# A fused attention and gated-MLP kernel on one core: the hand-written order of all engines replaced by another

## The chip, the core and the metric

The kernel runs on one core of a Trainium2 chip. The metric is device time in microseconds, from the first to the last instruction of an execution as the device counts it, median of several runs. Engines are named as in the profile: PE (TensorE) multiplies matrices, DVE (VectorE), ACT (ScalarE) and POOL (GpSimd) work on elements, SP (SyncE) issues DMA transfers. Each engine executes its own instructions in the order in which the program lists them, and waits on semaphores where it needs another's result.

## What is computed

A block-wise linear attention with decay for 4 batches, 8 heads, 768 tokens and head width 64, and behind it a gated MLP with a spatial projection. Cut to what matters:

```python
# attention: per head, blocks of 64 tokens, state kv carried from block to block
intra = ((qb @ kb.T) * Dmask) @ vb
inter = (qb * lam_pow) @ kv
out   = intra + inter
kv    = lam_block * kv + (kb * rev_pow).T @ vb
# gMLP on x = attention output as (batch, 768, 512)
h    = relu(x @ w_in)                  # 512 -> 1024
u, v = h[..., :512], h[..., 512:]
v_n  = (v - mean(v)) / sqrt(var(v) + 1e-6)
v_s  = w_spatial @ v_n + b_spatial     # over the 768 tokens
y    = (u * v_s) @ w_out               # 512 -> 512
```

## The kernel before

The work is cut into 12 pieces n of 256 tokens, three to a batch (n = 0 to 2 are batch 0). A piece goes through the attention, is turned into the MLP's input and projected. When the three pieces of a batch are there, the spatial product of that batch can run, and then its output product. The kernel has no loop over this: a string `ORDER` lists 675 tokens, and for each the function of that name is called. The last letter says the engine (T PE, D DVE, A ACT, P POOL, S SP), the numbers say which piece, half or bank. As the tokens are listed, so each engine executes its share; the framework adds the semaphores where one token needs another's data or buffer. PSUM has 8 banks; most tokens name the bank they use, and bank 7 keeps the attention state.

```python
for token in ORDER.split():
    name, *args, e = token.split(".")
    ops[name](e, *map(int, args))
```

The tokens, in the order of the flow:
- LK, LQ, LV n (`load`, L193): one piece of k, q or v from HBM, 512 KB, by SP into one of three buffers. WI, WS (`w_in`, `w_sp`, L249 and L254, two halves each), WO (L258): weights, issued by POOL with conversion to bf16. BS (L261): the bias. GT (`after`, L245): POOL copies one element of a loaded piece, and so waits for its landing; it holds back the weights behind it.
- KM, QM (`decay`, L291): k or q times its decay, half a piece each, on DVE or POOL. QC, VC: conversion of q and v to bf16. In n = 0 to 4, TK and TQ (`tr`, L321) transpose k and q on PE and EK, EQ bring the result to SBUF (EQ with the decay, L335); later pieces go through DMA transposes by SP (DK, DQ; L304, L308) instead. EQ is written for DVE whatever its letter:

```python
def e_q(e, n, x, b):
    nc.vector.tensor_tensor(...)
```

- SC (L352) makes the scores on PE, MK (L357) masks them on DVE; KV (L369) adds to the state, SS copies it out; AV (L390, L399) makes the attention output; FN reads one element of it; EX brings it out as the MLP's input.
- PV (L424) and PU (L462) are the two halves of the first projection on PE; EV and EU (`relu`) their evictions. BN (L439, L440), RA (L444), RD (L449) and VN (L453) normalise v; VN is on DVE throughout, bf16 from SBUF to SBUF.
- WT (L474) transposes w_spatial on PE once, EW evicts it. GP puts the bias into a bank, PW (L488) adds the spatial product to it (32 tokens of 6 matmuls; each needs all six VN of its batch), GM (L494) multiplies by u. PO (L499) is the output product of 128 tokens, EO its eviction, ST its store; PH, EH and SH do the last such tile in halves.
- FL (`f_l`, L269): k matmuls of w columns on a constant tile into a bank that is written anew afterwards. They compute nothing that is used.

At the start, `lam` is brought in, LB, LN, LL, LX and LT make the decay factors from it, msk, mkc, idn, posk, pos and one make masks and constants.

In the order before, 86 fillers of 256 columns stand in 12 groups ahead of the first spatial product PW.0.0.0. The weights stand on POOL as WI.0 behind GT.1.1 (q of n = 1), WI.1 behind GT.1.2 (q of n = 2), WS.0 behind GT.2.1 (v of n = 1), WO behind GT.2.2 (v of n = 2), with KM, QC and VC between them. SP's queue begins K0, Q0, K1, Q1, V0, V1, Q2, K2, V2, BS, K3, Q3, V3, K4, Q4.

Of the kernel before, what the change touches and what calls it, by code (L numbers as in the profile page):

```python
# [36 lines left out]
KV.3.0.T SC.3.0.0.1.T MK.3.0.0.1.D SC.3.1.2.3.T MK.3.1.2.3.D GP.0.2.1.4.A PW.0.2.1.4.T TK.4.2.6.T QC.4.2.A
TQ.4.2.5.T EQ.4.2.5.D GM.0.2.1.4.D GP.0.3.1.0.A PW.0.3.1.0.T AV.3.0.1.2.T FN.3.1.2.D SS.3.0.A KV.3.1.T KM.5.1.P
EK.4.2.6.A SC.4.0.3.4.T GM.0.3.1.0.D KM.5.0.D DK.5.S AV.3.1.1.2.T EX.3.1.2.A EX.3.0.1.A SC.4.1.5.6.T
MK.4.1.5.6.D PO.0.2.0.T EO.0.2.0.A PO.0.4.2.T EO.0.4.2.D QM.5.1.P QM.5.0.D DQ.5.S VC.5.P PO.0.3.1.T PU.3.0.5.T  # L40
PV.3.1.6.T PV.3.0.0.T VC.4.A SS.3.1.D KV.4.0.T MK.4.0.3.4.D AV.4.0.2.3.T EV.3.0.0.D BN.3.0.D PO.0.5.4.T
EU.3.0.5.A SS.4.0.A KV.4.1.T EV.3.1.6.A BN.3.1.D LK.6.S KM.6.0.P FN.4.2.3.A AV.4.1.2.3.T EX.4.1.3.D SS.4.1.A
LV.6.S EX.4.0.2.A RA.3.A RD.3.D PO.0.1.0.T EO.0.1.0.A EO.0.3.1.A KV.5.0.T SC.5.0.5.6.T MK.5.0.5.6.D SC.5.1.2.3.T
MK.5.1.2.3.D SS.5.0.A PO.0.0.0.T EO.0.0.0.A LQ.6.S QM.6.0.P PV.4.1.1.T PV.4.0.5.T LK.7.S KM.7.0.P LQ.7.S
KM.6.1.D VN.3.0.D LQ.8.S DK.6.S EO.0.5.4.A AV.5.0.2.6.T FN.5.2.6.D PU.4.0.3.T EV.4.1.1.A EV.4.0.5.A QM.6.1.P
AV.5.1.2.6.T BN.4.0.D VC.6.A KV.6.0.T GP.1.2.0.0.D EX.5.0.2.D PU.4.1.4.T EU.4.0.3.A EX.5.1.6.A EU.4.1.4.A
VN.3.1.D BN.4.1.D PV.5.1.1.T EV.5.1.1.D RA.4.A RD.4.D BN.5.1.D PV.5.0.5.T LV.7.S EV.5.0.5.A BN.5.0.D RA.5.A
VN.4.1.D VN.4.0.D RD.5.D VN.5.0.D PU.3.1.2.T EU.3.1.2.A DQ.6.S QM.8.1.P QM.8.0.P VN.5.1.D KM.7.1.D DK.7.S
PU.5.0.3.T PU.5.1.6.T QM.7.1.D QM.7.0.D DQ.7.S PW.1.2.0.0.T EU.5.0.3.D SS.6.0.A GM.1.2.0.0.D LK.8.S LK.9.S
LV.8.S GP.1.3.1.4.A PW.1.3.1.4.T GP.1.0.0.1.A EU.5.1.6.A PW.1.0.0.1.T GM.1.3.1.4.D GM.1.0.0.1.D GP.1.0.1.5.A  # L50
PW.1.0.1.5.T GM.1.0.1.5.D GP.1.1.1.2.A PW.1.1.1.2.T SC.6.0.3.4.T MK.6.0.3.4.D SC.6.1.0.1.T MK.6.1.0.1.D
GP.1.2.1.6.A VC.7.A GP.1.3.0.5.A KV.6.1.T PW.1.3.0.5.T GM.1.3.0.5.D KM.8.1.P KM.8.0.P PW.1.2.1.6.T GP.1.1.0.3.A
SS.6.1.A PW.1.1.0.3.T GM.1.1.1.2.D GM.1.2.1.6.D AV.6.0.0.4.T FN.6.0.4.D KV.7.0.T SS.7.0.A SC.7.1.1.2.T
GM.1.1.0.3.D AV.6.1.0.4.T EX.6.1.4.A DQ.8.S SC.7.0.5.6.T DK.8.S KV.7.1.T PO.1.4.3.T EX.6.0.0.D PU.6.0.4.T
KM.9.0.P LV.9.S LQ.9.S EO.1.4.3.A SS.7.1.A QM.9.0.P MK.7.0.5.6.D EU.6.0.4.A MK.7.1.1.2.D PV.6.0.0.T LQ.10.S
LK.10.S QM.10.1.P QM.9.1.P KM.9.1.D VC.8.D EV.6.0.0.D PO.1.1.3.T EO.1.1.3.A LV.10.S PV.6.1.5.T EV.6.1.5.A
BN.6.1.D PO.1.5.6.T EO.1.5.6.A AV.7.0.1.4.T FN.7.1.4.A KV.8.0.T SS.8.0.A SC.8.0.2.3.T SC.8.1.5.6.T DK.9.S
LQ.11.S ST.0.1.S AV.7.1.1.4.T EX.7.0.1.A MK.8.0.2.3.D KM.10.0.P PU.6.1.0.T MK.8.1.5.6.D PO.1.0.1.T KM.10.1.P
QM.10.0.P EX.7.1.4.A PV.7.1.2.T VC.9.A DQ.9.S LK.11.S GP.2.2.0.3.A BN.6.0.D RA.6.A ST.0.0.S ST.1.4.S EV.7.1.2.A
AV.8.0.5.6.T KV.9.0.T PU.7.1.4.T FN.8.5.6.D AV.8.1.5.6.T SS.9.0.A KV.9.1.T GP.2.0.1.2.A EO.1.0.1.A BN.7.1.D  # L60
EU.6.1.0.D RD.6.D VN.6.0.D EU.7.1.4.A SS.9.1.A KM.11.0.P DK.10.S QM.11.1.P DQ.10.S LV.11.S ST.0.2.S EX.8.0.5.D
VN.6.1.D PO.1.2.1.T EX.8.1.6.A EO.1.2.1.A GP.2.1.0.0.D PV.7.0.4.T EV.7.0.4.A BN.7.0.D PV.8.1.5.T EV.8.1.5.A
RA.7.A BN.8.1.D RD.7.D ST.0.5.S PV.8.0.6.T EV.8.0.6.A BN.8.0.D RA.8.A PU.8.1.1.T VN.7.1.D RD.8.D VN.7.0.D
VN.8.0.D GP.2.0.0.4.A PU.8.0.5.T EU.8.0.5.A PU.7.0.6.T VN.8.1.D GP.2.2.1.5.A EU.7.0.6.A PW.2.0.1.2.T KM.11.1.P
GP.2.1.1.6.A GM.2.0.1.2.D EU.8.1.1.D PW.2.2.0.3.T GM.2.2.0.3.D GP.2.3.1.2.A PW.2.1.0.0.T GM.2.1.0.0.D
PW.2.3.1.2.T GM.2.3.1.2.D PW.2.2.1.5.T GM.2.2.1.5.D SC.9.0.0.1.T VC.10.A KV.10.0.T SS.10.0.A QM.11.0.P
MK.9.0.0.1.D SC.9.1.2.3.T GP.2.3.0.5.A DK.11.S PW.2.0.0.4.T GM.2.0.0.4.D MK.9.1.2.3.D PW.2.3.0.5.T GM.2.3.0.5.D
PW.2.1.1.6.T GM.2.1.1.6.D AV.9.0.0.1.T SC.10.0.2.3.T SC.10.1.4.5.T KV.10.1.T FN.9.0.1.D AV.9.1.0.1.T DQ.11.S
MK.10.0.2.3.D PO.2.2.6.T EO.2.2.6.D ST.1.1.S ST.2.2.S PO.2.5.2.T EX.9.1.1.A EX.9.0.0.A PV.9.0.3.T EV.9.0.3.D
MK.10.1.4.5.D EO.2.5.2.A PO.1.3.6.T EO.1.3.6.D PV.9.1.1.T EV.9.1.1.A BN.9.1.D SS.10.1.A PO.2.0.0.T EO.2.0.0.A  # L70
ST.2.0.S AV.10.0.3.4.T VC.11.P SC.11.1.5.6.T SC.11.0.1.2.T KV.11.0.T SS.11.0.D FN.10.3.4.A AV.10.1.3.4.T
ST.0.4.S EX.10.0.3.A EX.10.1.4.A PU.9.1.0.T MK.11.1.5.6.D BN.9.0.D PU.9.0.3.T MK.11.0.1.2.D PV.10.0.4.T
EV.10.0.4.A RA.9.A ST.0.3.S PO.2.3.5.T EO.2.3.5.A RD.9.D AV.11.0.1.6.T ST.1.5.S ST.2.5.S VN.9.1.D FN.11.1.6.D
PV.10.1.2.T EV.10.1.2.A EU.9.0.3.D BN.10.0.D AV.11.1.1.6.T EX.11.1.6.D ST.1.3.S ST.1.2.S BN.10.1.D VN.9.0.D
PO.2.1.4.T PU.10.0.5.T EX.11.0.1.A PV.11.1.2.T EO.2.1.4.A RA.10.A EU.9.1.0.A GP.3.3.0.3.D GP.3.3.1.6.A ST.1.0.S
EV.11.1.2.A BN.11.1.D PV.11.0.1.T EV.11.0.1.A GP.3.2.1.4.A BN.11.0.D RD.10.D VN.10.0.D RA.11.A PU.11.0.0.T
# [485 lines left out]
```

## Time and profile before

| | us |
|---|---|
| runs | 148.59, 149.34, 150.53 |
| median | 149.34 |
| span of the profiled execution | 147.9 |
| TensorE busy, fillers (L269) among it | 137.0, 13.8 |
| VectorE, ScalarE, GpSimd busy | 114.9, 82.1, 46.7 |
| first PW matmul (L488) starts | 36.4 |
| last matmul (L499) ends | 144.2 |

Busy time of TensorE includes overlapping of pipelined matmuls, so the distance from the start of one matmul to that of the next is the better price: 0.163 us for a PW matmul of 384 columns, 0.216 for 512 columns, 0.109 for 256. The forty slices show the DMA engines at nine tenths or more from 3.7 to 48 us, and less afterwards:

```profile
PE   4999899999199999999999899999999999999990
...
DVE  4458958988956998799998968797795899696720
ACT  3886635598066473786663367987424446742041
POOL 7594562019700080226041800780732000000000
PEclk9999999999999999999999999999999999999999
DMA  3999999999999005999998999999999579200524
```

Each digit is the busy share of 3.7 us in tenths. The dip of PE to 1 in the eleventh slice is the one long hole after the start.

### The profile page before, as it was taken

The numbers are of one execution on the slowest core, as the hardware profiler recorded it, in microseconds if no ns is written. First come the engines' busy times: TensorE is split into PE (matmuls) and PEld (weight loads), VectorE is DVE, ScalarE is ACT, GpSimd is POOL, SyncE is SP. The second block draws the span as 40 slices with busy tenths as digits, with TensorE's granted clock in tenths as the row PEclk, the third lists the DMA queues.
The fourth block names the chain that finished last, engine by engine and source line by source line (L and its number), as shares of the span: only waits on it lengthen the run. The fifth ranks groups of instructions, "written<-read, shape, count | busy, mean of one in ns | idle before, by whom it ended". The sixth has DMA issues, their size and how long they took to land.

```text
span 147.9 us, 4771 instructions
## 1 busy us (share of the span) xinstructions
PE 137.0 (93%) x2019; PEld 90.1 (61%) x2032; DVE 114.9 (78%) x216; ACT 82.1 (56%) x165; POOL 46.7 (32%) x59
## 2 busy tenths in 40 slices
PE   4999899999199999999999899999999999999990
...
DVE  4458958988956998799998968797795899696720
ACT  3886635598066473786663367987424446742041
POOL 7594562019700080226041800780732000000000
PEclk9999999999999999999999999999999999999999
DMA  3999999999999005999998999999999579200524
GB/s 95 347 347 345 231 279 219 217 295 289 242 246 274 5 20 135 278 334 251 198 216 242 244 139 337 339 197 260 296 250 173 181 295 340 81 0 4 206 101 189
DMA packets 58376, 32.30 MB, mean 218 GB/s; under 512 B 15858, under 2 KB 55282, under 8 KB 58354
## 3 DMA queue, kind: packets, MB, share of 16 engines
...
q0 software_dynamic: 2384, 2.75, 11.0%
...
q10 hardware_dynamic: 2, 0.00, 0.0%
...
## 4 chain that ended last, share of the span: by engine, by line
PE 81%; DVE 6%; ACT 4%; issue 4%; DMA 1%; POOL 1%; POOLq 0%
PE ps L488 21%; PE ps L424 13%; PE ps L499 12%; PE ps L462 11%; PE ps L269 6%; PE ps L399 4%; PE ps L352 4%; PE ps L369 4%; PE ps L321 3%; PE ps L390 2%; DVE a_sb L357 2%; DVE st L439 1%; DMA out_dram<-o_sb 1%; ACT uT L429 1%; ACT L220 1%
## 5 line engine op out<-in xcount | busy, mean ns | idle before, releaser
L488 PE MATMUL ps<-wt_sb,vn 128*128 128x384 bf16 x192 | 33.8, 326 | 3.0 <-DVE wt_sb L180 3.0
L291 POOL TENSOR_TENSOR kc<-k_in,lv 128x512 bf16<-128x512 f32 x18 | 19.1, 1072 | 39.2 <-DMA k_in<-in_k_dram 17.9
L357 DVE TENSOR_TENSOR a_sb<-ps,m 128x1024 bf16<-128x1024 f32 x24 | 28.7, 1215 | 2.6 <-PE ps L352 2.6
L488 PEld LDWEIGHTS <-vn 128*128 128x128 bf16 x192 | 18.2, 98 | 15.3 <-DVE vn L453 4.3
L462 PE MATMUL ps<-xT,win_sb 128*128 128x256 bf16 x192 | 23.5, 273 | 0.0
L424 PE MATMUL ps<-win_sb,xT 128*128 128x512 bf16 x92 | 22.6, 379 | 0.2
L499 PE MATMUL ps<-wout_sb,gT 128*128 128x512 bf16 x83 | 21.7, 380 | 0.7 <-issue 0.3
L494 DVE TENSOR_TENSOR gT<-ps,uT 128x384 bf16<-128x384 f32 x32 | 16.6, 550 | 6.3 <-PE ps L488 5.5
L462 PEld LDWEIGHTS <-win_sb 128*128 128x128 bf16 x192 | 18.1, 98 | 3.9
L439 DVE BATCH_NORM_STATS2 st<-vh 128x6 f32<-128x512 bf16 x24 | 16.5, 686 | 3.3 <-ACT vh L429 3.1
L178 ACT ACTIVATE ps<-bsp 128x384 f32<-128x384 f32 x26 | 12.5, 493 | 9.5 <-DVE gT L494 6.4
L291 POOL TENSOR_TENSOR qc<-q_in,lqn 128x512 bf16<-128x512 f32 x11 | 11.9, 1087 | 17.2 <-DMA q_in<-in_q_dram 10.3
L178 ACT ACTIVATE o_sb<-ps 128x512 f32<-128x512 f32 x18 | 10.5, 596 | 11.0 <-PE ps L499 10.4
L429 ACT ACTIVATE vh<-ps 128x512 bf16<-128x512 f32 x19 | 11.3, 595 | 8.8 <-PE ps L424 8.8
L269 PE MATMUL ps<-ones 128*128 128x256 bf16 x86 | 13.8, 309 | 2.0 <-DVE ones L265 1.5
L424 PEld LDWEIGHTS <-xT 128*128 128x128 bf16 x96 | 9.3, 98 | 9.5
L499 PEld LDWEIGHTS <-gT 128*128 128x128 bf16 x92 | 8.4, 98 | 9.1
L453 DVE TENSOR_SCALAR vn<-vh,mv,rstd 128x512 bf16<-128x512 bf16 x24 | 13.5, 592 | 0.2
L178 ACT ACTIVATE xT<-ps 128x512 bf16<-128x512 f32 x15 | 8.5, 595 | 7.4 <-PE ps L399 7.4
L178 ACT ACTIVATE s_sb<-ps 128x256 bf16<-128x256 f32 x17 | 6.5, 380 | 8.9 <-PE ps L369 8.8
L269 PEld LDWEIGHTS <-ones 128*128 128x128 bf16 x86 | 8.7, 109 | 4.3 <-DVE ones L265 1.5
L429 ACT ACTIVATE uT<-ps 128x512 bf16<-128x512 f32 x17 | 9.9, 588 | 1.7 <-PE ps L462 1.7
...
## 6 DMA issues: line engine op xcount, KB each, us to landing
...
bsp<-in_moe_b_spatial_dram SPq DMA_DIRECT2D x1, 384.0 KB, 14.2
```

The lines of the kernel that those rows point to most:

```text
L178: nc.scalar.activation(out=o, in_=i, func=AF.Copy)
L269: nc.tensor.matmul(out=bank(b)[:, 0:w], lhsT=ones[:, 0:P], rhs=ones[:, 0:w], start=(new == 1 and i == 0), stop=True, skip_group_check=True)
L291: vec(e).tensor_tensor(out=dst[n % NCA][:, u].rearrange("p u m o d -> p o (u m) d"), in0=src[n % NIN].rearrange("p (o u) m d -> p o u m d" ...
L357: nc.vector.tensor_tensor(out=a_sb[n % NA][:, i].rearrange("p o w j x -> p o w (j x)"), in0=ps[:, b0:b1 + 1:b1 - b0].rearrange("p o (w y) ...
L424: nc.tensor.matmul(out=bank(b), lhsT=x[:, slot(c, g)], rhs=win_sb[:, g, DH:DFF], start=(g == 0), stop=(g == NCH - 1))
L429: nc.scalar.activation(out=o, in_=i, func=AF.Relu)
L439: nc.vector.bn_stats(out=st6[p2][:, t], in_=vh[p2][:, t])
L453: vec(e).tensor_scalar(out=vn[p2][:, t], in0=vh[p2][:, t], scalar1=mv[p2][:, t, 0:1], scalar2=rstd[p2][:, t:t + 1], op0=ALU.subtract, op1= ...
L462: nc.tensor.matmul(out=pu[:, f2].rearrange("p (c x) -> p c x", c=2), lhsT=win_sb[:, g, f * P:(f + 1) * P], rhs=x[:, slot(0, g):slot(1, g) ...
L488: nc.tensor.matmul(out=bank(b)[:, 0:HW], lhsT=vn[bb % 2][:, s, f * P:(f + 1) * P], rhs=wt_sb[:, s, i * HW:(i + 1) * HW], start=False, stop ...
L494: nc.vector.tensor_tensor(out=gT[bb % 2][:, f, cols], in0=bank(b)[:, 0:HW], in1=uT[bb % 2][:, f, cols], op=ALU.mult)
L499: nc.tensor.matmul(out=bank(b), lhsT=gT[bb % 2][:, f, t * P:(t + 1) * P], rhs=wout_sb[:, f, :], start=(f == 0), stop=(f == NCH - 1))
```

## The change

Only the string `ORDER` changes. It lists the same operations, but for the fillers: 9 groups with 15 matmuls of 512 and 2 of 256 columns in place of 86 of 256. All the other tokens appear as often as before; their sequence, the banks and the engine letters of those that can run on several engines are new. On DVE, counted over the whole order: EU 7 to 11, EK 1 to 5, SS 3 to 7, EV 5 to 7, GP 6 to 8, QC 1 to 3, EO 5 to 6, VC 2 to 3, EX 9 to 5, FN 7 to 4, KM 6 to 5, QM 3 to 2, EW 3 to 2, EH 2 to 0. POOL gets KM 19 instead of 18, QM 12 instead of 11, VC 7 instead of 4, QC 3 instead of 5; ACT has the rest. Four EQ now carry the letter A.

SP's queue begins Q0, K0, Q1, K1, V0, K2, V1, Q2, V2, K3, Q3, BS, Q4, V3, K4. POOL's weights stand differently: WI.0 behind GT.1.1 and KM.1.0, WI.1 behind KM.1.1, VC.1 and KM.2.1, WS.0 behind GT.2.1 and GT.2.2, WS.1 behind VC.2, WO behind KM.3.1, QC.4.2 and VC.3.

The diff, cut to the beginning, the passage around batch 2's first PW, and the end:

```diff
-one.D lam.A LK.0.S msk.P mkc.D FL.6.256.0.1.T LB.0.T LN.0.A posk.P LL.D LX.A KM.0.0.D pos.P idn.P
-FL.11.256.1.1.T TK.0.0.1.T KM.0.1.P FL.5.256.2.1.T TK.0.1.2.T LQ.0.S QC.0.1.D TQ.0.1.3.T LT.0.A QC.0.0.P
-TQ.0.0.4.T EQ.0.0.4.D LT.1.A EQ.0.1.3.D LK.1.S KM.1.1.P FL.13.256.5.1.T TK.1.1.5.T EK.0.0.1.A SC.0.0.3.4.T
-EK.0.1.2.A LQ.1.S QC.1.0.P EK.1.1.5.A GT.1.1.P WI.0.P KM.1.0.D LV.0.S SC.0.1.0.1.T LV.1.S TK.1.0.6.T EK.1.0.6.A
-FL.1.256.2.0.T TQ.1.0.2.T LQ.2.S LK.2.S QC.1.1.P FL.11.256.5.0.T TQ.1.1.5.T MK.0.0.3.4.D EQ.1.0.2.D MK.0.1.0.1.D
-VC.0.A FL.3.256.6.0.T KV.0.0.T AV.0.0.3.6.T SS.0.0.A FN.0.3.6.A LV.2.S QC.2.1.P BS.S LK.3.S GT.1.2.P WI.1.P
-EQ.1.1.5.D SC.1.1.0.1.T SC.1.0.4.5.T MK.1.0.4.5.D KV.0.1.T SS.0.1.A KM.2.0.P GT.2.1.P WS.0.P LQ.3.S LT.2.A
-AV.0.1.3.6.T LV.3.S LK.4.S VC.1.D FL.13.256.2.0.T KV.1.0.T LQ.4.S SS.1.0.A FL.5.256.2.0.T KV.1.1.T KM.2.1.P
-LK.5.S MK.1.1.0.1.D AV.1.0.2.4.T QC.2.0.A TQ.2.1.5.T EX.0.1.6.D WS.1.P TQ.2.0.0.T EQ.2.0.0.D LQ.5.S VC.2.P
-FN.1.2.4.A AV.1.1.2.4.T LV.4.S EX.1.0.2.D EQ.2.1.5.D EX.1.1.4.A FL.13.256.1.0.T PV.1.0.1.T EX.0.0.3.D SS.1.1.D
-PV.0.1.6.T EV.0.1.6.A PV.1.1.0.T EV.1.1.0.A KM.3.0.P KM.3.1.P QC.3.2.P GT.2.2.P WO.P EV.1.0.1.D BN.1.0.D
-BN.0.1.D TK.2.0.2.T BN.1.1.D PV.0.0.5.T VC.3.P FL.3.256.4.0.T TK.2.1.4.T EK.2.1.4.D EK.2.0.2.A SC.2.0.0.1.T
-MK.2.0.0.1.D FL.2.256.3.0.T SC.2.1.3.4.T MK.2.1.3.4.D EV.0.0.5.A RA.1.A BN.0.0.D RA.0.A RD.1.D LV.5.S RD.0.D
-PU.1.0.6.T PU.1.1.2.T KV.2.0.T SS.2.0.A EU.1.0.6.A AV.2.0.0.1.T FN.2.0.1.D VN.0.0.D VN.0.1.D PU.0.1.3.T
-EU.0.1.3.A KM.4.0.P AV.2.1.0.1.T EX.2.0.0.A EX.2.1.1.D GP.0.0.0.4.A EU.1.1.2.A GP.0.0.1.5.A PU.0.0.6.T VN.1.1.D
-VN.1.0.D EU.0.0.6.D PV.2.0.3.T KM.4.1.P EV.2.0.3.A BN.2.0.D PV.2.1.0.T EV.2.1.0.A BN.2.1.D WT.0.0.1.T WT.1.0.2.T
-EW.1.0.2.A EW.0.0.1.D RA.2.A RD.2.D VN.2.0.D WT.2.0.6.T EW.2.0.6.D PU.2.0.3.T GP.0.2.0.0.A PU.2.1.2.T VN.2.1.D
-PW.0.0.0.4.T EU.2.0.3.A EU.2.1.2.A WT.1.1.1.T EW.1.1.1.A WT.2.1.6.T EW.2.1.6.A GP.0.3.0.3.D GM.0.0.0.4.D
...
-PW.3.1.0.4.T GM.3.3.1.6.D EU.10.0.5.A GM.3.0.1.2.D GM.3.1.1.1.D PH.3.5.0.0.T PH.3.5.1.6.T GM.3.1.0.4.D
-PO.3.3.5.T EO.3.3.5.D EH.3.5.0.0.D ST.3.3.S SH.3.5.0.S PO.3.4.2.T EO.3.4.2.D GP.3.0.0.1.A PW.3.0.0.1.T
-GP.3.2.0.4.A ST.3.4.S EH.3.5.1.6.D SH.3.5.1.S PW.3.3.0.3.T GM.3.3.0.3.D GM.3.0.0.1.D PW.3.2.0.4.T GM.3.2.0.4.D
-PO.2.4.5.T EO.2.4.5.A ST.2.4.S PO.3.0.0.T EO.3.0.0.A ST.3.0.S PO.3.1.2.T EO.3.1.2.A ST.3.1.S PO.3.2.6.T
-EO.3.2.6.A ST.3.2.S
+lam.A msk.P mkc.D LB.1.T LN.1.A LQ.0.S LK.0.S idn.P LQ.1.S posk.P one.D pos.P FL.5.512.0.1.T LK.1.S LL.D LX.A
+QC.0.0.P QC.0.1.D LV.0.S TQ.0.0.3.T KM.0.1.D LT.0.A TK.0.1.0.T EK.0.1.0.A EQ.0.0.3.A LK.2.S KM.0.0.D TQ.0.1.1.T
+QC.1.1.P FL.1.512.4.1.T LV.1.S EQ.0.1.1.D LT.1.A GT.1.1.P QC.1.0.D TK.0.0.1.T SC.0.1.3.5.T EK.0.0.1.D
+FL.2.512.2.1.T KM.1.0.P MK.0.1.3.5.D LQ.2.S TQ.1.0.4.T SC.0.0.1.2.T WI.0.P FL.3.512.6.1.T VC.0.A MK.0.0.1.2.D
+EQ.1.0.4.D TQ.1.1.6.T KM.1.1.P LV.2.S FL.1.512.5.0.T TK.1.0.0.T FL.1.256.5.0.T EQ.1.1.6.A KV.0.0.T EK.1.0.0.D
+LT.2.A AV.0.0.4.5.T SC.1.0.0.1.T LK.3.S SS.0.0.D KV.0.1.T KM.2.0.D FN.0.4.5.D MK.1.0.0.1.D VC.1.P TK.2.0.2.T
+LQ.3.S TK.1.1.3.T AV.0.1.4.5.T KM.2.1.P EK.1.1.3.D EX.0.1.5.A SS.0.1.D SC.1.1.0.1.T FL.1.256.5.0.T WI.1.P
+MK.1.1.0.1.D TK.2.1.6.T FL.2.512.3.0.T KV.1.0.T AV.1.0.3.5.T EX.0.0.4.D SS.1.0.A GT.2.1.P QC.2.1.A KV.1.1.T
+QC.2.0.D FL.1.512.0.0.T EK.2.1.6.D TQ.2.1.0.T BS.S TQ.2.0.1.T FN.1.3.5.D EK.2.0.2.D EQ.2.1.0.A AV.1.1.3.5.T
+LQ.4.S EQ.2.0.1.D SS.1.1.A SC.2.1.0.6.T EX.1.0.3.D EX.1.1.5.A SC.2.0.1.4.T PV.0.0.2.T GT.2.2.P WS.0.P
+MK.2.1.0.6.D PV.1.1.3.T EV.0.0.2.A VC.2.P MK.2.0.1.4.D PV.0.1.0.T WS.1.P BN.0.0.D KV.2.0.T AV.2.0.2.4.T LV.3.S
+SS.2.0.A EV.0.1.0.D PV.1.0.6.T BN.0.1.D PU.0.0.5.T EV.1.0.6.A KM.3.1.P EV.1.1.3.D FN.2.2.4.A AV.2.1.2.4.T
+BN.1.1.D PU.0.1.1.T EX.2.0.2.A EX.2.1.4.A BN.1.0.D PV.2.0.0.T KM.3.0.D PU.1.0.6.T EV.2.0.0.A RA.1.A WT.0.0.3.T
+GT.1.2.P EU.0.1.1.D EU.0.0.5.D EU.1.0.6.A PV.2.1.2.T EW.0.0.3.A BN.2.0.D WT.1.0.0.T RA.0.A TK.3.2.3.T EV.2.1.2.A
+RD.0.D EW.1.0.0.D RD.1.D LK.4.S WT.2.0.1.T EK.3.2.3.A PU.2.0.5.T VN.0.1.D BN.2.1.D EW.2.0.1.A WT.2.1.6.T
+WT.0.1.4.T VN.0.0.D EU.2.0.5.A PU.2.1.3.T VN.1.1.D RA.2.A GP.0.1.0.2.A RD.2.D PU.1.1.1.T VN.2.0.D LK.5.S
+QC.3.2.A VN.2.1.D VN.1.0.D EU.2.1.3.D EW.2.1.6.A QC.4.2.P PW.0.1.0.2.T GP.0.0.0.3.D LV.4.S TQ.3.2.5.T EW.0.1.4.A
+GM.0.1.0.2.D PW.0.0.0.3.T GP.0.2.0.2.D VC.3.P EQ.3.2.5.D WT.1.1.0.T TQ.4.2.6.T GM.0.0.0.3.D WO.P LQ.5.S
+EW.1.1.0.D KV.3.0.T EQ.4.2.6.A PW.0.2.0.2.T SS.3.0.D LK.6.S KM.4.1.P GP.0.3.1.3.A EU.1.1.1.D SC.3.0.5.6.T
+GP.0.1.1.1.A GM.0.2.0.2.D SC.3.1.0.4.T KV.3.1.T GP.0.3.0.2.D PW.0.1.1.1.T MK.3.1.0.4.D PW.0.3.0.2.T KM.4.0.P
+KM.5.1.P MK.3.0.5.6.D GP.0.0.1.0.A PW.0.3.1.3.T KM.5.0.P SS.3.1.D GP.0.2.1.6.A GM.0.1.1.1.D VC.4.D TK.4.2.5.T
...
+VN.7.1.D PO.1.5.3.T RD.8.D VN.8.0.D VN.8.1.D PW.2.2.0.1.T EO.1.5.3.A ST.1.5.S QM.11.0.P PW.2.1.0.5.T ST.0.3.S
+DQ.10.S EU.8.0.6.D EU.6.1.0.D GM.2.2.0.1.D PW.2.1.1.2.T QM.11.1.P SS.9.1.A GP.2.2.1.1.A EU.8.1.4.D GP.2.3.1.0.A
+GM.2.1.0.5.D LV.11.S SC.9.0.3.4.T KV.10.0.T SC.9.1.5.6.T MK.9.0.3.4.D PW.2.3.1.0.T KM.11.0.P KM.11.1.P
+GP.2.3.0.3.D GP.2.0.0.4.A PW.2.2.1.1.T DK.11.S GM.2.1.1.2.D MK.9.1.5.6.D PW.2.0.0.4.T GM.2.3.1.0.D PW.2.3.0.3.T
+GP.2.0.1.5.A GM.2.0.0.4.D SS.10.0.A PW.2.0.1.5.T GM.2.3.0.3.D GM.2.2.1.1.D AV.9.0.3.4.T GM.2.0.1.5.D KV.10.1.T
+FN.9.3.4.D SC.10.1.1.2.T SC.10.0.0.6.T MK.10.0.0.6.D AV.9.1.3.4.T DQ.11.S PO.2.5.5.T EX.9.1.4.A MK.10.1.1.2.D
+EX.9.0.3.A PO.1.3.4.T EO.2.5.5.A VC.11.D PU.9.0.0.T EO.1.3.4.A SS.10.1.D ST.1.3.S PV.9.1.4.T EU.9.0.0.A
+AV.10.0.0.5.T KV.11.0.T SC.11.0.1.6.T FN.10.0.5.A EV.9.1.4.A SC.11.1.2.3.T AV.10.1.0.5.T MK.11.0.1.6.D SS.11.0.A
...
+GP.3.3.0.4.A RD.11.D VN.10.1.D EU.10.0.2.A PU.10.1.1.T VN.9.0.D VN.11.1.D EO.2.2.5.A VN.10.0.D VN.11.0.D
+PW.3.3.0.4.T EU.10.1.1.A GP.3.0.0.6.D ST.1.2.S ST.2.2.S EU.11.1.3.D GP.3.0.1.2.A ST.2.1.S PW.3.0.0.6.T
+GP.3.1.1.5.A ST.2.0.S GP.3.2.1.1.A GP.3.3.1.3.A ST.2.5.S PW.3.1.1.5.T GM.3.0.0.6.D PW.3.3.1.3.T GM.3.1.1.5.D
+PW.3.1.0.0.T PW.3.0.1.2.T PW.3.2.1.1.T GM.3.0.1.2.D GM.3.3.1.3.D GM.3.1.0.0.D GP.3.2.0.6.A PW.3.2.0.6.T
+GM.3.2.1.1.D PO.3.4.5.T GM.3.2.0.6.D PO.3.3.6.T EO.3.4.5.D GM.3.3.0.4.D PO.3.1.2.T ST.3.4.S EO.3.3.6.A ST.2.4.S
+ST.3.3.S PO.3.0.4.T EO.3.1.2.D PO.3.2.5.T ST.3.1.S EO.3.0.4.D PH.3.5.1.1.T ST.3.0.S EO.3.2.5.A PH.3.5.0.6.T
+EH.3.5.1.1.A ST.3.2.S EH.3.5.0.6.A SH.3.5.1.S SH.3.5.0.S
```

74 lines of the change are left out of this document (30 added, 44 removed).

## The prediction

> **What bounds the kernel now.** I read the page first (busy time, the forty slices, the chain of waits), then the waits of TensorE, a table of windows, and the timeline around the longest wait.
>
> ```profile
> PE 137.0 (93%) x2019; PEld 90.1 (61%) x2032; DVE 114.9 (78%) x216; ACT 82.1 (56%) x165; POOL 46.7 (32%) x59
> ...
> PE 81%; DVE 6%; ACT 4%; issue 4%; DMA 1%; POOL 1%; POOLq 0%
> ...
> L269 PE MATMUL ps<-ones 128*128 128x256 bf16 x86 | 13.8, 309 | 2.0 <-DVE ones L265 1.5
> ```
>
> TensorE is the bound, but part of its 137.0 us is the filler FL (L269): 86 matmuls on a constant, 13.8 us. The windows (columns: length, then busy time of PE, PEld, DVE, ACT, POOL, then clock and DMA) show where it has slack:
>
> ```profile
> 20.00:24.00 4.00, 3.95 (x47) 2.58 (x45) 3.51 (x7) 0.90 (x2) 0.90 (x2) 1.00 1.19 229
> ...
> 28.00:32.00 4.00, 4.00 (x90) 3.16 (x89) 3.47 (x10) 2.23 (x6) 0.00 (x0) 1.00 1.14 246
> ...
> 36.00:40.30 4.30, 1.34 (x11) 0.81 (x9) 4.28 (x3) 1.27 (x3) 3.56 (x4) 1.00 1.03 260
> 40.30:50.00 9.70, 9.70 (x131) 6.76 (x131) 6.44 (x12) 5.21 (x8) 0.00 (x0) 1.00 0.83 207
> ```
>
> From 40.3 us to its last matmul at 144.2 us it lacks only about 1.2 us. Before that there is one hole, 36.0 to 40.3, with VectorE marked busy throughout. From 20 to 36 VectorE is busy 14.2 of 16 us: there it is VectorE that feeds TensorE.
>
> ```profile
> 35.73 0.79 POOL L258 DMA_DIRECT2D wout_sb<-in_moe_w_out_dram  x1
> ...
> 36.02 3.70 DVE L453 TENSOR_SCALAR vn<-vh,mv,rstd 128x512 bf16<-128x512 bf16 x1
> ...
> 36.52 1.05 POOL L182 CAST vb<-v_in 128x1024 bf16<-128x1024 f32 x1
> ...
> 37.52 2.04 POOL L291 TENSOR_TENSOR kc<-k_in,lv 128x512 bf16<-128x512 f32 x2
> 39.64 0.55 DVE L180 COPY wt_sb<-ps 128x768 bf16<-128x768 bf16 x1
> 40.24 0.32 PE L488 MATMUL ps<-wt_sb,vn 128*128 128x384 bf16 x1 [2.96 <-DVE wt_sb L180]
> ```
>
> That hole is VN.2.0: an operation that takes 0.38 to 0.41 us elsewhere took 3.70, ending when POOL's run (WO, VC.3, KM.4.0, KM.4.1) ended. The first spatial product, begun at 36.4, waited 3.28 us from matmul to matmul for it. The time before is thus: PW starts 36.4, PE work from there 103.5, this hold 3.3, other idle 1.2, from the last matmul to the end 3.7; 148.1 against a span of 147.9 (I carry the -0.2). The runs' median, 149.34, is 1.44 above the span.
>
> The PE work is priced by start-to-start rows of the chain: 6 matmuls of L488 0.97 us, 4 of L424 or L499 0.86, 8 of L462 0.87, 32 of L352 0.45, 16 of L369 0.25, 16 of L399 0.22 and 8 of L390 0.11, a transpose 0.056. Over the order this makes 123.5 us in both kernels. Ahead of the first PW stand 20.0 us before and 21.1 after, so 103.5 and 102.4 are left.
>
> **Fillers.** 22016 filler columns become 8192, 11.1 us (17 matmuls at 0.213, 69 at 0.109) become at most 7. All lie before 27 us. What they may gain is a shorter wait of VectorE for scores and transposes, so it is inside the 7.6 us of VectorE waits below and is not counted again. What they also do is speed TensorE up:
>
> ```profile
> 4.05 2.53 PE L269 MATMUL ps<-ones 128*128 128x256 bf16 x11
> ...
> 9.03 1.58 PE L269 MATMUL ps<-ones 128*128 128x256 bf16 x13
> ```
>
> Start to start this is 0.213 us a matmul in the first row, 0.109 in the second, though the granted-clock column says 1.00 for both. With fewer fillers the fast pace may come later. The Trainium skill, "TensorE: Matmul & The Clock Gate", Part 1, says the clock is halved by default, released by about 3.4 us of sustained activity and halved again after an idle window; by that rule removing fillers costs time. The two rows agree with the first half of it; no row shows a return to the slow pace. It becomes a rival below.
>
> **VectorE before the first PW.** Up to batch 0's last VN the new order holds 53 VectorE steps instead of 45. Changes by kind and mean: EK +4 (0.425), KM +2 (0.69), QC +2 (0.68), EV +1, EU +1 (0.68 each), SS +1 (0.42), FN +1 (0.14), EX -2, VC -1 (0.68), EW -1 (0.54): +3.8 us, from 29.1 to 32.9. The four EQ marked A change nothing: e_q always calls VectorE. Back to back, operations overlap slightly (busy total 114.9 against 119.7 summed), so x0.96: +3.6. Before, without the hold, the last VN would have ended at 36.02 + 0.38 + 0.55 + 0.38 = 37.3. From 4 to 36 us VectorE waited 7.6 of 32 us. If the new order waits as much, VN ends at 40.9; if the extra work all goes into those waits, at 37.3. I take the middle, 39.1, and PW at 39.2: fillers no longer delay scores and transposes that VectorE waits for, but startup waits (LN, LX, K and Q landing) stay.
>
> **POOL against VN.** POOL's new run is KM.3.1, QC.4.2, VC.3, WO, KM.4.1, KM.4.0. Q4, V3 and K4 are now the 13th to 15th transfers of SP's queue, and before these landed at 35.5, 37.0 and 38.5. So QC.4.2 (1.03) comes near 35.5, VC.3 (1.04) near 37, WO (0.79) at 38.1, KM.4 (2 x 1.05) from 38.9. That lies on the six VN (36 to 39). Held VN took 1.17 and 0.87 us at 67.6 and 96.6 behind one POOL operation, 3.70 here. Bounds: 0 to 3.3; I take one POOL operation, 1.0, nearest to the two smaller cases. The Trainium skill, "SBUF — State Buffer", Who interferes with whom, has the port pair that VectorE and GpSimd share locked for one whole instruction. By that a hold ends within one POOL operation, 1.05 us; the two small cases agree, the 3.70 row does not, and the trace decides for the range.
>
> **Weights and loads.** WI.0 stays near 10.6. WI.1 goes behind VC.1 and KM.2.1 (some 17 instead of 14.8). WS.0 goes behind GT.2.2, a wait for V2, which landed at 24.5; so 24.7 instead of 18.3, and WS.1 behind VC.2, 26.7 instead of 20.1. With the old 10.5 to 12.3 us to landing, WS.1 lands at 37.2 to 39.0; at the pace its queue had (3.6 us a piece, 2 us to start) at 34. WT.2.1 stands 2.4 us of PE work ahead of PW: PW at 36.4 to 41.4. I take it as hidden behind 39.2 and put the 2.2 us in the range; queued behind WT.2.1 on TensorE would be PU.2.1, PU.1.1 and all PW. BS falls behind K3 and Q3 but GP needs it only near 38. Late, SP keeps ST.1.5 ahead of DQ.10, LV.11, DK.11, DQ.11: PO.1.5 is the last work ahead of PW.2, which comes 59.8 us of PE work after PW.0, so they begin near 102, and SC.10, the first to need them, stands 9 us of PE work behind PW.2's start. DQ.11 must follow AV.9.1; 4.1 us of PE work (PO.2.5, PO.1.3, PU.9.0, PV.9.1, AV.10.0, KV.11.0) cover its 2.7 to 5.9 us, so 0 to 1.8; I take 0.
>
> **After the first PW.** From PW.0 to PO.0.2 VectorE has 14.2 x 0.96 = 13.6 us for 12.8 of TensorE: +0.8. Later stages are TensorE-heavy as before (16.6 against 15.7, 13.3 against 12.7, 16.4 against 14.6), so the old 1.2 idle stays. At the end EO.3.4 stands ahead of GM.3.3.0 on VectorE: GM.3.2.1 is ready 0.3 after PE wants it, and PO.3.1 waits 0.4: +0.7. The last output is a half tile (0.38 eviction instead of 0.60): 3.5 behind the last matmul. Other share changes after PW sit beside TensorE and cost 0; if PSUM banks come free late, the most that I bound is one eviction (0.68) in each of four batches, 2.7, and no gain.
>
> Sum: 39.2 + 1.0 + 102.4 + (1.2 + 0.8 + 0.7) + 3.5 - 0.2 = 148.6 span, + 1.44 = **150.0 us**.
>
> **Rivals.**
> - Slower, POOL's hold: VN ends unabsorbed at 40.9 and POOL's run, now fed by WO and KM.4 right behind VC.3, holds one VN as long as before (3.3): 44.2 + 102.4 + 2.7 + 3.5 - 0.2 = 152.6, 154.0 us. It decides from a first PW at 42.6 on (150.9 span). For it: the same row has happened. Against: loads 1.49 us apart leave gaps.
> - Faster: the hold vanishes and the waits absorb all: 37.3 + 102.4 + 1.2 + 3.5 - 0.2 = 144.2, 145.6 us. For it: TensorE's 3.28 us hole was one collision. Against: it needs VectorE with no loss in a load-bound stage.
> - Slow pace: TensorE stays at 0.213 until PV. The 11.6 us ahead of PV become 22.6, PV at 26.7, PW at 40.2: 151.0 us. For it: 63% fewer filler columns. Against: at the slow pace TensorE is nearly always busy, as it was when the pace rose.
> - The change doesn't do what it says: only for EQ, whose letters are idle; its price stands above.
>
> **Numbers.** Forecast 0.37, faster 0.18, POOL's hold or late banks and weights together 0.35, slow pace 0.10. The range reaches from near the faster case to the slower one: 146 to 154.5; the likeliest case alone 148 to 152. About 2% is what a measurement of this kernel tells from no change: under 146.35 is faster (0.18, its own case), above 152.33 slower (0.35), and forecast and slow pace lie between (0.47).
>
> **What would show it.** First L488 matmul near 39 to 41; VectorE about 90% busy from 10 to 39 with TensorE holes there; a VN above 0.6 us under POOL; TensorE lacking 2 to 4 us after that. A first PW before 37 or a long hold breaks the forecast; so do holes of over 3 us late, which I would have to seek in banks or transposes.

## The result and the profile after

The changed kernel took 160.14 us (median of 4, 159.56 to 160.92); before, measured beside it, 149.38. The ratio is 1.072, with a 95% interval of [1.067, 1.078]: 7% slower. Its profiled execution has a span of 158.9 us against 147.9. All ratios here leave out runs that took over 1.5% longer than the fastest run of the same kernel.

The page's totals of the changed kernel, and two of its groups (busy us, mean ns of one, then the idle time of the engine just before them and who ended most of it). The change takes away some lines ahead of these functions, so the mask `m_k` is L356 here, the spatial product L487, VN L452:

```profile
PE 134.1 (84%) x1945; PEld 85.3 (54%) x1963; DVE 117.6 (74%) x224; ACT 74.1 (47%) x154; POOL 50.2 (32%) x62
...
L487 PE MATMUL ps<-wt_sb,vn 128*128 128x384 bf16 x192 | 33.8, 326 | 6.5 <-DVE a_sb L356 4.4
L356 DVE TENSOR_TENSOR a_sb<-ps,m 128x1024 bf16<-128x1024 f32 x24 | 29.0, 1221 | 13.7 <-PE ps L398 4.8
```

In the kernel before, the mask's group read:

```profile
L357 DVE TENSOR_TENSOR a_sb<-ps,m 128x1024 bf16<-128x1024 f32 x24 | 28.7, 1215 | 2.6 <-PE ps L352 2.6
```

One mask takes as long as ever (1.22 us), but VectorE stood idle 13.7 us ahead of masks instead of 2.6, 11.1 of it for works that are not the scores (4.8 for AV, L398; the rest for PW, PV and PO), and TensorE's spatial products waited 4.4 us for masks, with which they share no data. The mask's share of the chain of waits rose from 2% to 10%. TensorE's forty slices (3.97 us each) show where:

```profile
PE   2789696988595988799996699999996879999990
```

The windows (columns as before) with the gaps of TensorE:

```profile
24.00:28.00 4.00, 2.49 (x26) 1.03 (x24) 2.47 (x3) 0.68 (x2) 1.17 (x2) 1.00 1.14 259
...
40.30:50.00 9.70, 7.13 (x112) 4.65 (x111) 8.82 (x19) 2.80 (x5) 2.47 (x3) 1.00 0.75 171
...
80.00:90.00 10.00, 7.01 (x177) 4.69 (x178) 6.28 (x8) 3.21 (x9) 5.08 (x5) 1.00 0.78 224
```

Between 80 and 90 us TensorE lacks 3 us while VectorE is busy 6.3 of 10: neither is the bound there, they wait in turn. The timeline of that passage:

```profile
80.90 1.15 PE L487 MATMUL ps<-wt_sb,vn 128*128 128x384 bf16 x6
81.05 1.23 DVE L356 TENSOR_TENSOR a_sb<-ps,m 128x1024 bf16<-128x1024 f32 x1 [0.23 <-ACT s_sb L177]
82.30 0.49 ACT L177 ACTIVATE ps<-bsp 128x384 f32<-128x384 f32 x1 [1.36 <-DVE a_sb L356]
82.32 1.14 PE L487 MATMUL ps<-wt_sb,vn 128*128 128x384 bf16 x6 [0.27 <-DVE a_sb L356]
83.57 1.23 DVE L356 TENSOR_TENSOR a_sb<-ps,m 128x1024 bf16<-128x1024 f32 x1 [0.83 <-PE ps L487]
84.84 1.14 PE L487 MATMUL ps<-wt_sb,vn 128*128 128x384 bf16 x6 [1.39 <-DVE a_sb L356]
```

Against the order these are PW.1.3.1.0 (bank 0), MK.6.1.1.4, GP.1.2.0.4, PW.1.0.0.3, MK.6.0.2.6 and PW.1.2.0.4. MK.6.1.1.4 reads banks 1 and 4, and PW.1.0.0.3, in bank 3, starts as it ends. MK.6.0.2.6 reads banks 2 and 6; its scores have been there since 81.0, but it starts only when PW in bank 3 has ended, and PW in bank 4 starts only when it has. In none of these three waits do the two sides share a bank. (GP.1.2.0.4, which waits for MK.6.1.1.4 too, does share bank 4 with it.) PW.1.3.1.0 in bank 0, outside 1 to 4, runs beside the first mask, which stands ahead of it in the order, without waiting for it. By the trace the PW at 84.84 waits on the semaphore that VectorE's instructions raise, so the wait is one that the framework wrote into the program. What joins the works is a line that the diff does not touch:

```python
in0=ps[:, b0:b1 + 1:b1 - b0].rearrange("p o (w y) -> p o w y", w=2),   # m_k
```

One VectorE operation reads both banks of scores by a stride. In the kernel before, all 24 masks name two neighbouring banks. In the changed order 13 of 24 do not: (3,5), (0,6), (1,4), (0,4), (1,4), (0,3), (0,5), (1,4), (2,6), (1,5), (3,6), (0,6) and (1,6). Theory W: such a mask counts as touching every bank from the first to the last, so that works in the banks between and the mask wait for one another. Rival V: the loss lies in the stage ahead of the first PW, in VectorE's work, the loads and POOL's hold on VN, and the rest follows from that.

The passage around the first PW, VectorE's VN and then POOL's run beside them:

```profile
36.96 1.25 DVE L452 TENSOR_SCALAR vn<-vh,mv,rstd 128x512 bf16<-128x512 bf16 x1
...
38.94 2.40 DVE L452 TENSOR_SCALAR vn<-vh,mv,rstd 128x512 bf16<-128x512 bf16 x2
...
41.45 1.06 DVE L452 TENSOR_SCALAR vn<-vh,mv,rstd 128x512 bf16<-128x512 bf16 x3
```

```profile
37.02 1.04 POOL L181 CAST vb<-v_in 128x1024 bf16<-128x1024 f32 x1 [0.47 <-DMA v_in<-in_v_dram]
38.00 0.79 POOL L257 DMA_DIRECT2D wout_sb<-in_moe_w_out_dram  x1
38.81 2.05 POOL L290 TENSOR_TENSOR kc<-k_in,lv 128x512 bf16<-128x512 f32 x2
```

Two VN were held (1.25 us, and 2.08 for the first of the pair), and the first PW matmul began at 41.1, its third, behind the last VN, at 42.6.

### The profile page after: what moved, and what is told of

It is laid out like the page before. It is cut to its first block, busy times and chain, and to the rows that moved or that the text cites. A ratio compares the mean times of both kernels' runs of the same rounds, so it can differ in the third digit from the quotient of the medians.

```text
span 158.9 us, 4625 instructions
## 1 busy us (share of the span) xinstructions
PE 134.1 (84%) x1945; PEld 85.3 (54%) x1963; DVE 117.6 (74%) x224; ACT 74.1 (47%) x154; POOL 50.2 (32%) x62
## 3 DMA queue, kind: packets, MB, share of 16 engines
q0 software_dynamic: 2384, 2.75, 10.0%
## 4 chain that ended last, share of the span: by engine, by line
PE 65%; DVE 20%; ACT 5%; DMA 4%; issue 3%; SPq 0%; POOL 0%; DVEq 0%; ACTq 0%
PE ps L487 17%; PE ps L423 12%; PE ps L461 11%; DVE a_sb L356 10%; PE ps L498 10%; PE ps L351 4%; PE ps L398 3%; DVE vn L452 3%; PE ps L320 3%; DMA q_in<-in_q_dram 3%; PE ps L368 2%; PE ps L389 2%; DVE gT L493 1%; DMA out_dram<-o_sb 1%; PE ps L268 1%
## 5 line engine op out<-in xcount | busy, mean ns | idle before, releaser
L487 PE MATMUL ps<-wt_sb,vn 128*128 128x384 bf16 x192 | 33.8, 326 | 6.5 <-DVE a_sb L356 4.4
L356 DVE TENSOR_TENSOR a_sb<-ps,m 128x1024 bf16<-128x1024 f32 x24 | 29.0, 1221 | 13.7 <-PE ps L398 4.8
L487 PEld LDWEIGHTS <-vn 128*128 128x128 bf16 x192 | 18.3, 98 | 19.3 <-issue 5.5
L290 POOL TENSOR_TENSOR kc<-k_in,lv 128x512 bf16<-128x512 f32 x19 | 20.5, 1088 | 24.6 <-PE ps L368 18.0
L177 ACT ACTIVATE xT<-ps 128x512 bf16<-128x512 f32 x19 | 11.0, 596 | 21.1 <-PE ps L398 17.3
L177 ACT ACTIVATE ps<-bsp 128x384 f32<-128x384 f32 x24 | 11.4, 489 | 16.2 <-DVE a_sb L356 8.9
L438 DVE BATCH_NORM_STATS2 st<-vh 128x6 f32<-128x512 bf16 x24 | 16.4, 682 | 2.4 <-ACT vh L428 2.3
L177 ACT ACTIVATE o_sb<-ps 128x512 f32<-128x512 f32 (+1 forms) x19 | 10.7, 573 | 12.5 <-PE ps L498 12.1
L423 PEld LDWEIGHTS <-xT 128*128 128x128 bf16 x96 | 8.8, 98 | 11.1 <-issue 1.7
L428 ACT ACTIVATE vh<-ps 128x512 bf16<-128x512 f32 x17 | 10.0, 594 | 9.5 <-PE ps L423 7.0
L181 POOL CAST vb<-v_in 128x1024 bf16<-128x1024 f32 x7 | 7.3, 1039 | 17.4 <-issue 7.6
L452 DVE TENSOR_SCALAR vn<-vh,mv,rstd 128x512 bf16<-128x512 bf16 x24 | 11.3, 512 | 0.3
L398 PE MATMUL ps<-a_sb,vb 64*64 64x128 bf16 x384 | 10.3, 217 | 0.0
L351 PE MATMUL ps<-qT,kT 64*64 64x128 bf16 x384 | 9.6, 226 | 0.4 <-DVE kT L179 0.4
L428 ACT ACTIVATE uT<-ps 128x512 bf16<-128x512 f32 x13 | 7.6, 593 | 4.0 <-PE ps L461 4.0
## 6 DMA issues: line engine op xcount, KB each, us to landing
bsp<-in_moe_b_spatial_dram SPq DMA_DIRECT2D x1, 384.0 KB, 10.6
```

Of the source, the lines that this page charges most:

```text
L177: nc.scalar.activation(out=o, in_=i, func=AF.Copy)
L290: vec(e).tensor_tensor(out=dst[n % NCA][:, u].rearrange("p u m o d -> p o (u m) d"), in0=src[n % NIN].rearrange("p (o u) m d -> p o u m d" ...
L351: nc.tensor.matmul(out=pa[o][row(c), w, j], lhsT=kT[n % NTR][row(o), u, j, c * Q64:(c + 1) * Q64], rhs=qv(n, o, u, c), start=(w == 0 and j ...
L356: nc.vector.tensor_tensor(out=a_sb[n % NA][:, i].rearrange("p o w j x -> p o w (j x)"), in0=ps[:, b0:b1 + 1:b1 - b0].rearrange("p o (w y) ...
L423: nc.tensor.matmul(out=bank(b), lhsT=x[:, slot(c, g)], rhs=win_sb[:, g, DH:DFF], start=(g == 0), stop=(g == NCH - 1))
L428: nc.scalar.activation(out=o, in_=i, func=AF.Relu)
```

## The experiments

**Wide masks taken away, and put in.** Three kernels: the changed order with its 13 wide masks split into two operations of one bank each; the kernel before with all 24 masks split so (the condition is then always true); and the kernel before with its banks 0 to 6 renamed, which makes all 24 pairs wide (two to four banks between) and moves nothing else.

```diff
 def m_k(e, n, i, b0, b1):
+        if b1 - b0 > 1:
+            for o, b in enumerate((b0, b1)):
+                nc.vector.tensor_tensor(
+                    out=a_sb[n % NA][:, i, o].rearrange("p w j x -> p w (j x)"),
+                    in0=bank(b).rearrange("p (w y) -> p w y", w=2),
+                    in1=m01.rearrange("p j m x -> p (j m x)").unsqueeze(1).broadcast_to((P, 2, 2 * P)),
+                    op=ALU.mult)
+        else:
```

```diff
 kernel before: banks 0 1 2 3 4 5 6 -> 2 5 1 6 3 0 4 in every token, pairs in rising order
-MK.0.0.3.4.D ... MK.0.1.0.1.D ... MK.1.0.4.5.D
+MK.0.0.3.6.D ... MK.0.1.2.5.D ... MK.1.0.0.3.D
```

> Theory W (span of banks): the mask MK reads two banks with one access, and what lies in the banks between them counts as touched, so that MK waits for all earlier work there and all later work there waits for MK. In the changed kernel 13 of 24 masks read banks that are not neighbours. Split here into two operations of one bank each, the TensorE holes behind them (some 13 us summed from matmul to matmul; a_sb has 15.9 us of the chain against 2.3 before) should go: 148 to 151 us, a ratio of 0.99 to 1.01 to the kernel before. Rival V (VectorE is simply loaded more, and its holds by GpSimd cost the time): no better than 159 to 161 us, since the split only adds VectorE work.

> The kernel before with all 24 masks split in two, its pairs being neighbours: the price of the split alone. W and V both: VectorE has 24 more operations of about 0.1 us overhead each (2.4 us), most of it beside TensorE: 149 to 151 us. If it gains over 1 us, a pair of neighbours also holds something back and W is not the whole of it.

> The kernel before with its seven banks renamed, and nothing else: all 24 masks then read banks with two or three others between them. W: slower by 8 to 20 us (24 wide masks in place of the 13 that cost about 10): 157 to 170 us, with TensorE holes of 1.2 to 1.7 us behind masks. V: names of banks mean nothing, 149 to 150 us.

Measured, with the kernel before at 148.98 us beside them: 147.65 (147.03 to 148.11) for the split changed order, 149.89 for the split kernel before, 189.02 (188.35 to 189.60) for the kernel before with wide pairs. The split kernel before took 149.52 to 150.41 in three runs and 145.51 in one, the kernel before itself 148.29 to 150.84 in six and 146.00 in one: set side by side, splitting neighbouring pairs gains at most 0.5 us. W holds against V on both sides: 12.5 us go when the wide masks go, and 40 us come where only bank numbers make masks wide, more than either theory expected. In that last kernel one mask still takes 1221 ns; the longest waits of TensorE (us in total, times, longest) are for masks and for a bias that ScalarE brings in:

```profile
PE ps L484 <- ACT ps L174: 5.9, 2, 3.0
PE ps L420 <- DVE a_sb L353: 5.8, 2, 3.3
PE ps L495 <- DVE a_sb L353: 5.0, 4, 2.1
PE ps L348 <- DVE a_sb L353: 3.7, 3, 1.4
```

Projections (L420), output products (L495), scores (L348): whatever comes next in a bank between. The bias (GP, L174) ahead of the PW (L484) waits for masks in its turn, 12.7 us in all by ScalarE's waits.

Not all of the 40 us is waiting. By the two pages TensorE is idle 38.4 us of the span instead of 10.9, and busy 149.2 us instead of 137.0 with the same matmuls: 27.5 us of holes and 12.2 us of slower work. The granted clock was 0.93 to 0.94 in the mean of each of the four runs (0.99 to 1.00 in the kernel before). In the trace it is half in seven stretches of 3.41 us between 32 and 162 us; half of these 23.9 us is close to the 12.2, and neither theory had priced it.

**Neighbouring banks without splitting.** The split kernel leaves a rival: that halves free their banks earlier. So the changed order was given other bank numbers, worked out so that all 24 pairs are neighbours, with no token moved and no mask split.

```diff
-SC.6.1.1.4.T ... SC.6.0.2.6.T MK.6.1.1.4.D PW.1.3.1.0.T PW.1.0.0.3.T ... GP.1.2.0.4.A ... MK.6.0.2.6.D ... PW.1.2.0.4.T
+SC.6.1.2.3.T ... SC.6.0.4.5.T MK.6.1.2.3.D PW.1.3.1.6.T PW.1.0.0.1.T ... GP.1.2.0.0.A ... MK.6.0.4.5.D ... PW.1.2.0.0.T
```

> The changed order, with the banks dealt out anew so that each of the 24 masks reads two neighbouring banks in one operation, as before; nothing is split, and no token moves. Theory W (a mask on banks that are not neighbours counts as touching all banks between them, so works of those banks wait for one another): 146.0 to 148.5 us, like the version with split masks (147.65) or a little under it, since 13 VectorE operations fewer are issued. Rival S (what helped there was the splitting itself: the halves free their banks earlier): masks are whole again, so 152 to 160 us.

146.92 us (146.83 to 147.65), ratio to before 0.986 [0.980, 0.991]: W, and not the splitting. The passage that was quoted above, in this kernel (the spatial product is L483, the mask L352):

```profile
73.36 2.44 PE L483 MATMUL ps<-wt_sb,vn 128*128 128x384 bf16 x14
...
74.36 1.21 DVE L352 TENSOR_TENSOR a_sb<-ps,m 128x1024 bf16<-128x1024 f32 x1
```

The second mask of n = 6 now runs beside the products instead of between them, and both PW (73.7 and 74.7; the 14 matmuls are the last two of PW.1.3.1.6 and all twelve of theirs) follow without a hole.

**Half of them.** The changed order with the masks split only from n = 6 on.

```diff
+        if n >= 6 and b1 - b0 > 1:
```

> The changed order; of its 13 masks on banks that are not neighbours only the six of n = 6 to 11 are split, the seven of n = 0 to 5 stay. If each mask costs what the hole of TensorE behind it shows in the changed kernel's trace (1.65, 0.60, 1.71, 1.55, 1.54, 1.61 us after 60 us, 8.7 in all): 151.5 us, 150.5 to 152.5. If every one of the 13 costs alike (12.5 / 13 = 0.96 us): 154.4, 153.5 to 155.5. If the lost time lies all ahead of the first spatial product: 159 to 160.

153.91 us (153.62 to 154.43), 6.2 under the changed kernel. That rules out that all the lost time lies ahead of the first PW, and it fits a like share for each mask (154.4). The sum by holes took off too much: the hole at 62.8 us belongs to MK.5.1, which was left wide and still has its 1.65 us, and a distance from matmul to matmul holds the matmul itself. TensorE's idle time in the other five, 0.27, 1.39, 1.33, 1.32 and 1.39 us, is 5.7 and gives 154.4 too, so this run does not tell the two ways of counting apart. From 80 to 140 us TensorE is busy without a gap:

```profile
60.00:80.00 20.00, 18.57 (x304) 11.98 (x302) 15.34 (x35) 12.63 (x28) 6.27 (x7) 1.00 1.13 266
80.00:100.00 20.00, 20.00 (x378) 12.26 (x370) 16.51 (x31) 9.82 (x24) 11.04 (x11) 1.00 0.85 241
```

**POOL's hold on VN.** Three kernels. First the kernel before with the issue of WO, which stood ahead of VC.3 on POOL, behind KM.4.1.

```diff
-GT.2.2.P WO.P ... VC.3.P ... KM.4.0.P ... KM.4.1.P
+GT.2.2.P ... VC.3.P ... KM.4.0.P ... KM.4.1.P WO.P
```

> The kernel before with WO moved on GpSimd's queue behind KM.4.1, so that the 3.7 us VN no longer meets the issue of a weight load. If the issue of WO is what keeps VN waiting through three further operations: the hold shrinks to one operation, 1 us or less, and the time falls by 2 to 2.7 us to 146.7 to 147.5. If any run of GpSimd operations keeps it waiting: 0 to 0.8 us less, 148.5 to 149.5.

148.15 us (146.29 to 148.20), between the two expectations, so it tells nothing of WO. The profiled execution is the run of 146.29; its VN took 0.55 and 0.84 us. In the kernel before with split masks, where POOL's queue had WO in its old place, VN.2.0 took 0.41 and VN.2.1 0.66; in the kernel with 24 wide masks one VN took 3.73. The length of the hold differs from case to case by what meets what.

Then POOL was kept idle beside the VN: in the order with neighbouring banks, QC.4.2 and VC.3 went to ScalarE; in the kernel before, VC.3 to ScalarE and KM.4 to VectorE, behind the last VN.

```diff
 order with neighbouring banks
-QC.4.2.P ... VC.3.P
+QC.4.2.A ... VC.3.A
 kernel before
-VC.3.P ... KM.4.0.P ... KM.4.1.P
+VN.2.1.D KM.4.0.D KM.4.1.D ... EU.2.1.2.A VC.3.A
```

> The order with neighbouring banks, and the conversions QC.4.2 and VC.3, which POOL runs beside the normalisations VN of batch 0, on ScalarE instead. Theory P (POOL's run still holds VN, for the 1.0 us that the prediction put on it): first PW 0.7 to 1.2 us earlier, 145.2 to 147.2, that is 0.5 to 1.2 under the version with them on POOL. Rival N (the hold is not on the path, or ScalarE is late for RA and the evictions instead): within 0.5 us of it, or slower by up to 1.5.

> The kernel before, with POOL kept idle beside VN.2.0 and VN.2.1 (but for the issue of WO): VC.3 on ScalarE behind EU.2.1, KM.4.0 and KM.4.1 on VectorE behind VN.2.1. If the 3.3 us hold of VN in its profile is POOL's run of VC.3, KM.4.0 and KM.4.1: both VN take 0.38 to 0.45 us, the hole of TensorE at the first PW falls from 3.3 to under 0.6 us, and the time to 145.5 to 147.5 us. If something else holds VN (the loads, the semaphores): the hole stays over 1 us and the time at 148.5 to 150.

The first took 146.24 us (145.92 to 146.74; ratio to before 0.980 [0.976, 0.984]): 0.7 less than with the two on POOL, inside P's range, but its first PW came 0.3 us earlier (37.0 after 37.3) and not the 0.7 to 1.2 of P. All six VN run at their short duration:

```profile
34.45 0.40 DVE L448 TENSOR_SCALAR vn<-vh,mv,rstd 128x512 bf16<-128x512 bf16 x1
...
35.58 0.70 DVE L448 TENSOR_SCALAR vn<-vh,mv,rstd 128x512 bf16<-128x512 bf16 x2
...
36.82 1.06 DVE L448 TENSOR_SCALAR vn<-vh,mv,rstd 128x512 bf16<-128x512 bf16 x3
```

What the hold cost can't be read from these 0.7 us. The last three VN began later than before (36.8 after 36.2), and PW's third matmul, which waits for the last of them, came only 0.2 us earlier (37.9 after 38.1); 0.45 of the 0.67 us between the two spans lies behind the last matmul (3.61 after 4.06). The edit also let POOL issue WO 12.8 us earlier (25.1 after 37.9).

The second shows the hole of the kernel before gone: both VN take 0.41, and the first PW matmuls follow one another.

```profile
36.32 0.41 DVE L449 TENSOR_SCALAR vn<-vh,mv,rstd 128x512 bf16<-128x512 bf16 x1
...
37.11 0.41 DVE L449 TENSOR_SCALAR vn<-vh,mv,rstd 128x512 bf16<-128x512 bf16 x1
...
36.76 1.14 PE L484 MATMUL ps<-wt_sb,vn 128*128 128x384 bf16 x6
```

Its span is 144.6 against 147.9, the 3.3 us of that hole. Its ratio to before is 0.976 [0.968, 0.983], from two of its four runs (146.29, the one with the trace, and 145.21). The other two took 148.77 and 148.67, at granted clocks of 0.997 and 1.000, and what made them longer is not shown. Nor does this trace alone prove that POOL was the cause: the hole is also down to 0.4 us or less in the traces of the two other kernels with the old order above, WO late and masks split, where POOL kept its run.

The thirteen traces together do show it. Of their 312 VN, 254 have no POOL instruction beside them, and these took 0.38 to 0.42 us without exception. Of the 58 that have one, 30 took 0.48 to 3.73. So no VN is held without POOL; why some are held through one POOL instruction, some through three and some not at all stays open.

**The slow pace.** In the order with neighbouring banks, first 2.69 times as many filler columns in the same places (40 matmuls of 512 and 6 of 256, 22016 columns as in the kernel before), then, with QC.4.2 and VC.3 on ScalarE, three fillers in a gap alone.

```diff
-FL.5.512.1.1.T ... FL.1.512.3.1.T ... FL.2.512.1.1.T ... FL.3.512.1.1.T ...
+FL.13.512.1.1.T ... FL.3.512.3.1.T ... FL.5.512.1.1.T ... FL.8.512.1.1.T ...
 the second kernel
-TQ.0.0.0.T KM.0.1.D
+TQ.0.0.0.T FL.3.512.2.1.T KM.0.1.D
```

> The order with neighbouring banks, and 43 filler matmuls of 512 columns and 6 of 256 in place of 15 and 2: 2.75 times as many columns in the same nine places, about as many as the kernel before has. Theory G (TensorE's slow pace, which lasted to about 14 us in the changed kernel, costs time ahead of the first PW, as the rival in the prediction had it): the pace rises near 8 us, and the time falls by 0.5 to 1.5 us. Rival F (that stage is set by VectorE and the loads): no gain; the fillers are in the way while TensorE is slow, 0 to +3 us.

> The order with neighbouring banks and QC.4.2 and VC.3 on ScalarE (146.24 us in its own runs), and three filler matmuls of 512 columns more, put behind TQ.0.0, where TensorE idled 1.25 us from 5.9 us on; nothing else moves. Theory G (the slow pace costs time ahead of the first PW): the run of TensorE from 3.5 us on is then unbroken, the pace rises near 7 us instead of 10 to 11 and does not fall back near 18, and the first PW comes 0.3 to 1.0 us earlier: 145.2 to 146.0. Rival F (VectorE, ScalarE and the loads set that stage): first PW within 0.3 us of 37.0, and 145.9 to 146.7.

The 43 and 2.75 in the first expectation are a miscount; the kernel has the 40 named above. The first kernel took 153.12 us (151.31 to 153.95), worse than both theories allow. In its profiled execution, the longest of its four (153.95), the pace did rise early (0.427 us a filler until 6.4 us, 0.217 from 6.8 on), but the first PW came at 38.8 instead of 37.3, its VN then met POOL's KM.4 and took 2.18 us, and TensorE stood 2.0 us at 88 us for a transposed k. Behind the hole of 2.2 us that the held VN left at 39.3, the pace fell back as well: PW matmuls came 0.32 us apart instead of 0.163, and the granted clock was 0.62 from 40 to 44 us. So it says that fillers in the way cost, and nothing clean of the pace.

The second took 145.78 us (145.75 to 145.78 in three runs, 148.34 in one; ratio 0.976 [0.972, 0.979]), 0.5 under the same kernel without the three fillers. The fillers in its timeline, start, length and count:

```profile
3.48 2.32 PE L264 MATMUL ps<-ones 128*128 128x512 bf16 x5
...
6.01 1.33 PE L264 MATMUL ps<-ones 128*128 128x512 bf16 x3
7.18 0.39 PE L316 MATMUL ps<-ident,kc 128*128 128x128 bf16 x4
```

A group of four transposes takes 0.39 us from 7.2 on, where it took about 0.6 until 11 us before. The first PW matmul did not come earlier (37.15, as F has it), but the last VN ended at 36.9 instead of 37.9, so the 0.75 us from PW's second matmul to its third are 0.17 again. The time fits G, 0.1 us from F's range; the place is PW's wait and not its start.

**Two waits more.** With the same kernel, transposes and EK of a piece that is there were put ahead of one that waits for K2, and RA.1 ahead of EV.2.0.

```diff
-KM.2.0.D ... TK.2.0.6.T ... TK.1.1.5.T AV.0.1.4.3.T ... EK.1.1.5.D
+TK.1.1.5.T EK.1.1.5.D KM.2.0.D ... AV.0.1.4.3.T TK.2.0.6.T
-EV.2.0.0.A RA.1.A
+RA.1.A EV.2.0.0.A
```

> The kernel a_pace with two places of its order changed ahead of the first PW: TK.1.1, AV.0.1 and EK.1.1 ahead of the transposes TK.2.0 and of KM.2.0, which wait for K2 (TensorE idled 1.3 us there, from 14.2 us on), and RA.1 with its table load ahead of EV.2.0 on ScalarE (VectorE waited 1.5 us for RA's result near 33). If these two waits are on the path to the first PW: PW 0.8 to 2.0 us earlier than in a_pace, 143.5 to 145.3 us. If the path goes through VectorE's total of work or the loads: within 0.5 us of a_pace.

145.79 us (145.70 to 145.91), ratio to before 0.976 [0.973, 0.978], the same as without these two edits, which is the second reading of the expectation. The wait ahead of TK.2.0 only moved: TensorE then stood 1.55 us ahead of AV.0.1. This version and the one before it beat both kernels, by 2.4% and by 9%.

## Why the prediction failed

Forecast 150.0, measured 160.14. Its steps against the changed kernel's profile, and against the same order with neighbouring banks:

| us | forecast | changed | neighbouring banks |
|---|---|---|---|
| first PW starts | 39.2 | 41.1 | 37.3 |
| wait of PW for VN | 1.0 | 1.2 | 0.5 |
| TensorE's work from there | 102.4 | 102.4 | 102.4 |
| other idle time up to the last matmul | 2.7 | 10.6 | 0.9 |
| last matmul to the end | 3.5 | 3.6 | 4.1 |
| span | 148.6 | 158.9 | 145.2 |

(The work of 102.4 is the forecast's price in all three columns, and the idle time is what the measured span then leaves over; the forecast sum carries -0.2 besides.)

- **The step that failed** is the last sentence on the time after the first PW: "if PSUM banks come free late, the most that I bound is one eviction (0.68) in each of four batches, 2.7". The sum of the forecast adds nothing for it. The banks cost 13.2 us (160.14 to 146.92; 12.5 by the split masks): of the span's 13.7, 3.8 lie ahead of the first PW, 0.7 in its wait and 9.7 after it, less 0.5 at the end. It bounded a bank that is freed late by its own eviction. What happened was a wait between banks that have nothing to do with each other, which no row of the profile before could show, since all pairs were neighbours there; the quoted line of `m_k` and the bank numbers in the diff could have raised the question. Without it the same sum is 3.1 us too high (150.0 against 146.92): in the span 1.9 ahead of the first PW, 0.5 in the hold and 1.8 of idle time, less 0.6 behind the last matmul.
- **VectorE ahead of the first PW** was sized too high: with neighbouring banks the last VN ended at 38.1, of which 0.76 is a hold, so 37.3. That is the lower of the two bounds (37.3 to 40.9); the 3.6 us of work that were added went into waits altogether, not by half.
- **POOL's hold** was forecast at 1.0. With neighbouring banks one VN was held 0.76 us, and PW's wait was 0.5. In the changed kernel two VN were held, 0.85 and 1.68 us beyond their 0.40: the first until VC.3 ended, the second through both KM.4, which it met because it came late (38.9). So the hold of 1.68 lasted over two POOL instructions and not one. The rival built on it (154.0) had the meeting right, but it was a consequence of the late VN.
- **The slow pace** was priced at 1.0 us as a rival and is worth about 0.5 by that run, which lies at the edge of what these runs tell apart. TensorE's transposes were slow to 11 or 12 us with neighbouring banks. In the changed kernel, where the wide masks leave more holes, the clock's record in the trace begins only at 15.3 us, against 8.3 in the kernel before.
- **Loads and weights**: WS.1 landed at 35.0, inside 34 to 39. With neighbouring banks TensorE waited for no DMA transpose late, as taken.
- **The work of TensorE** and the end fit: in the changed kernel's trace TensorE is idle 11.6 us from the first PW to its last matmul, against the 1.2 and 10.6 of the table. Of the signs named, "holes of over 3 us late, which I would have to seek in banks" pointed the right way, but the holes were nine of 0.6 to 1.7 us, seven of them ended by a mask. The first PW (41.1) came at the late end of the 39 to 41 that were named, but TensorE lacked 10.6 us after it instead of 2 to 4.
- **The faster rival** (145.6) is near what the order does without wide masks (146.92 and 147.65): its sign was right for the order, and the bank numbers turned it.

The Trainium skill, "PSUM — Partial Sum Buffer", PSUM bank collisions raise a hardware error, asks for guards on PSUM by bank (or quadrant of a bank), not by address. The runs agree that a mask of neighbouring banks needs no more than that; the guards that the program got for 13 strided masks were wider than a bank, and 12.5 to 13.2 us is what the width cost.
